# The last output tile of a gated-attention and MLP kernel, split at column 288 instead of column 192

## The chip, the cores and the metric

The kernel runs on one core of one Trainium2 chip. The metric is the device time of one execution in microseconds. A core has five engines that run side by side and wait for each other through semaphores: TensorE (PE in the profile; its weight loads are shown apart as PEld) multiplies matrices into PSUM, VectorE (DVE), ScalarE (ACT) and GpSimd (POOL) work on tiles, and SyncE (SP) here only issues DMA transfers. ACT and POOL can issue transfers too. A transfer is cut into packets that 16 DMA engines move.

## The reference

Two stages follow each other. The first is a linear attention with a decaying state, for 4 batches, 8 heads, 768 steps and a head size of 48; the second is an MLP on the 3,072 rows that come out of it, with 384 model columns, 2,048 hidden columns and a gate h * cos(h):

```
for t in range(S):
    state = alpha[:, :, t, :, None] * state + np.einsum('bhd,bhe->bhde', k[:, :, t], v[:, :, t])
    y[:, :, t] = np.einsum('bhd,bhde->bhe', q[:, :, t], state)
...
x = np.ascontiguousarray(attn_out.transpose(0, 2, 1, 3)).reshape(B * S, H * D)
...
h = x @ w_in
g = h * np.cos(h)
return (g @ w_out).astype(np.float32)
```

The output is 3,072 by 384 in fp32. Matrices are multiplied in bf16 and summed in fp32.

## The kernel before

The 3,072 rows are worked in 12 pairs of 128-row chunks (J = 0 to 11, three pairs a batch). For each pair the attention steps (sums of the logarithms of alpha, scaled q and k, transposes, scores, mask, outer products, the running state, and the output `yT`) make x transposed in bf16, and then the MLP follows in three kinds of steps:

- `mlp1` (the matmuls at L360) makes the hidden layer in four pieces of 512 columns in PSUM. `cosine` (L366, on ACT) and `gate` (L371, on DVE) turn each piece into bf16 tiles `gsb`, with the hidden columns on the partitions.
- `mlp2` (L389) multiplies the 16 blocks of 128 hidden columns with `w2` and sums them into one PSUM tile of 128 rows by 384 columns for each chunk c = 0, 1 of a pair. The step is split into four parts of four blocks each, so that a part can start as soon as its piece of the gate is there. Each matmul has a 128x128 block of `gsb` as its stationary weights, which PEld loads before it, and streams columns of `w2`.
- `evict_o` (L401) copies the tile out of PSUM on ACT or DVE, and `store` (L407) issues its transfer to the output on SP's queue, 1,536 bytes a row.

The very last tile, (J, c) = (11, 1), is made otherwise. It lies in two PSUM tiles of different banks, `o_last`, with half the columns each. Each part of `mlp2` runs its four blocks for the first half and then the same four blocks for the second (L381 to L384), so the block of weights is loaded once for each half. `evict_o` copies the first half on ACT and the second on DVE (L397), and `store` issues the first on ACT's own queue and the second on SP's.

The order of the work is written out by hand. `PLAN` gives each step of each pair a time, the steps are sorted by it, and every engine and every queue carries out its share in that order. Times in `PLAN` only order the steps. For the end of the program they give, on TensorE, for pair 11: `m2 0 1`, `m2 1 1`, `m2 0 2`, `m2 0 3`, `m2 1 2`, `m2 1 3` (chunk, part), so the last 16 matmuls are the parts 2 and 3 of the last tile. Then come `evo 0`, `out 0`, `evo 1` and `out 1`. After the last store SP waits for all outstanding transfers, and a closing exchange of semaphores between the engines ends the program.

Two other places are used below for their durations: `cums` and `cums0` end in matmuls of only two columns (L168), each with a weight block of 128x128, and the inputs are loaded with rows of 384 bytes.

Of the kernel before, what the change touches and what calls it, by code (L numbers as in the profile page):

```python
# [9 lines left out]
FP = mybir.dt.float32  # L10
# [6 lines left out]
def kernel(  # L17
# [10 lines left out]
    nc = tc.nc  # L28
    B, H, S, D = q.shape
    DM, DF = moe_w_in.shape  # L30
    C = 128
# [16 lines left out]
    sb = ctx.enter_context(tc.tile_pool(name="sb", bufs=2))  # L48
# [31 lines left out]
    for lst, nm, n in ((lna_t, "lna", NL), (kh_t, "kh", NQ), (qh_t, "qh", NQ), (vp_t, "vp", NV)):  # L80
        for r in range(n):
            t = consts.tile([C, 2, H, 64], BF, tag=f"{nm}{r}", name=f"{nm}{r}")
            nc.vector.memset(t[:, :, :, D:64], 0.0)
            lst.append(t)
    for r in range(NS):
        t = consts.tile([C, 2, H, 64], BF, tag=f"vs{r}", name=f"vs{r}")
# [8 lines left out]
    w2 = consts.tile([C, NF, DM], BF, tag="w2", name="w2")  # L95

    a_sb, kqv, cp_sb, icp_sb, qkT_sb, A_sb, c2_sb = {}, {}, {}, {}, {}, {}, {}
    xT, gsb = {}, {}
# [73 lines left out]
    def two_banks(name):  # L172
        return ps.tile([C, 2, 512], FP, tag="h", name=name, bufs=3)
# [179 lines left out]
    h_ps, c_sb, o_ps, o_sb = {}, {}, {}, {}  # L353
# [17 lines left out]
        nc.vector.tensor_tensor(out=gsb[J][:, u * FW : (u + 1) * FW], in0=h_ps.pop((J, u)), in1=c_sb.pop((J, u)),  # L371
                                op=ALU.mult)

    HALVES = [slice(0, DM // 2), slice(DM // 2, DM)]

    def mlp2(J, c, part):
        if (J, c) == (NJ - 1, 1):
            if part == 0:

                o_ps[J, c] = [ps.tile([C, 512], FP, tag="x", name="o_last", bufs=1), two_banks("o_last")[:, 0]]  # L380
            for z, cols in enumerate(HALVES):  # L381
                for ft in range(part * NF // MP, (part + 1) * NF // MP):
                    nc.tensor.matmul(o_ps[J, c][z][:, 0 : DM // 2], gsb[J][:, ft, c * C : (c + 1) * C], w2[:, ft, cols],  # L383
                                     start=(ft == 0), stop=(ft == NF - 1))  # L384
            return
        if part == 0:
            o_ps[J, c] = ps.tile([C, 512], FP, tag="o", name="o_ps", bufs=1)
        for ft in range(part * NF // MP, (part + 1) * NF // MP):
            nc.tensor.matmul(o_ps[J, c][:, 0:DM], gsb[J][:, ft, c * C : (c + 1) * C], w2[:, ft],  # L389
                             start=(ft == 0), stop=(ft == NF - 1))  # L390

    def evict_o(J, c, copy):
        if (J, c) == (NJ - 1, 1):
            o_sb[J, c] = []
            for z, cp in enumerate((nc.scalar.copy, nc.vector.tensor_copy)):
                t = sb.tile([C, DM // 2], FP, tag=f"o_half{z}", name="o_half", bufs=1)
                cp(out=t, in_=o_ps[J, c][z][:, 0 : DM // 2])  # L397
                o_sb[J, c].append((t, HALVES[z], (nc.scalar, nc.sync)[z]))
        else:
            t = sb.tile([C, DM], FP, tag="o_sb", name="o_sb", bufs=4)  # L400
            copy(out=t, in_=o_ps.pop((J, c))[:, 0:DM])  # L401
            o_sb[J, c] = [(t, slice(0, DM), nc.sync)]
# [8 lines left out]
    def idle(n):  # L411
# [13 lines left out]
        "evT": lambda J, c, eng="DVE": evict_T(J, c, copies[eng]), "scores": scores, "mask": mask, "outer": outer,  # L425
        "add": add_state, "state": decay_state, "yT": yT, "evy": lambda J, c, eng="ACT": evict_y(J, c, copies[eng]),
        "m1": mlp1, "sin": cosine, "gate": gate, "m2": mlp2, "evo": lambda J, c, eng="ACT": evict_o(J, c, copies[eng]),
        "out": store, "idle": idle,
    }
# [73 lines left out]
    for key, line in PLAN.items():  # L503
        kind, *rest = key.split()
        for J, word in enumerate(line.split()):
            if word != "-":
                t, _, eng = word.partition(":")
# [38 lines left out]
```

## Time and profile before

| | us |
|---|---|
| median of 3 runs | 184.79 |
| lowest and highest | 184.72, 184.88 |
| the profiled execution | 185.2 |
| its span, from the first to the last instruction | 183.4 |
| PE, DVE, ACT, POOL busy | 177.0, 128.4, 129.4, 80.3 |
| mlp1 matmuls L360 (576), mlp2 matmuls L389 (368) | 67.1, 67.4 |
| the last tile's 32 matmuls L383 | 3.1 |
| its copies L397 on ACT and on DVE | 0.32, 0.36 |

The profile is of one execution. A line of a group names the source line, the engine, the operation and the tiles as out<-in, then shapes and count; after the bar stand the busy time in us, the mean duration of one in ns, and the idle time before them with what ended it. Matmuls overlap, so the mean of one (246 ns at L383) is longer than the step from one to the next, which is read from the chain: so many us for so many matmuls. The chain is followed back from the last instruction, at each step to what released it. A view in order of time gives start and duration of each instruction or run of like instructions; SPq and ACTq are the queues' issues of transfers. The granted TensorE clock was 1.000 throughout.

### The profile page before, as it was taken

The numbers are of one execution on the slowest core, as the hardware profiler recorded it, in microseconds if no ns is written. First come the engines' busy times: TensorE is split into PE (matmuls) and PEld (weight loads), VectorE is DVE, ScalarE is ACT, GpSimd is POOL, SyncE is SP. The second block draws the span as 40 slices with busy tenths as digits, with TensorE's granted clock in tenths as the row PEclk, the third lists the DMA queues.
The fourth block names the chain that finished last, engine by engine and source line by source line (L and its number), as shares of the span: only waits on it lengthen the run. The fifth ranks groups of instructions, "written<-read, shape, count | busy, mean of one in ns | idle before, by whom it ended". The sixth has DMA issues, their size and how long they took to land.

```text
span 183.4 us, 5752 instructions
## 1 busy us (share of the span) xinstructions
PE 177.0 (96%) x2473; PEld 132.8 (72%) x2473; DVE 128.4 (70%) x174; ACT 129.4 (71%) x168; POOL 80.3 (44%) x114
## 2 busy tenths in 40 slices
PE   7999999989999999989999999999999999999993
PEld 2444889664797876966789769776786796788772
DVE  7268879179889696689539985988569759074650
ACT  3665769698599989869798999659947173551531
POOL 5357500568687756562991099345075111000000
DMA  6999999999988999989228970571652300020122
GB/s 151 261 261 198 215 211 249 246 267 287 247 197 201 262 242 230 256 189 285 59 46 211 282 212 4 138 176 32 168 162 65 98 5 0 5 86 4 43 86 86
DMA packets 57801, 29.47 MB, mean 161 GB/s; under 512 B 50992, under 2 KB 56496, under 8 KB 57776
## 3 DMA queue, kind: packets, MB, share of 16 engines
q1 hardware_dynamic: 56256, 25.86, 57.7%
q0 software_dynamic: 1376, 3.15, 9.1%
q8 instruction: 19, 0.31, 0.7%
q10 hardware_dynamic: 144, 0.10, 0.2%
q14 instruction: 6, 0.05, 0.1%
HBM read 25.17 MB, written 4.72 MB: 163 GB/s over the span
## 4 chain that ended last, share of the span: by engine, by line
PE 87%; ACT 8%; DMA 2%; DVE 1%; issue 1%
PE h_ps L360 34%; PE o_ps L389 31%; PE y_ps L339 5%; PE A_ps L273 4%; PE idle_ps L415 3%; PE T_ps L259 3%; PE U_ps L290 2%; DMA a<-in_alpha_dram 2%; ACT c_sb L366 2%; ACT lna L142 2%; PE o_last L383 1%; ACT cp L201 1%; PE cums_h L156 1%; PE cums L156 1%; ACT icp L193 1%; ACT L137 1%
## 5 line engine op out<-in xcount | busy, mean ns | idle before, releaser
L371 DVE TENSOR_TENSOR gsb<-h_ps,c_sb 128x1024 bf16<-128x1024 f32 x48 | 58.1, 1222 | 24.1 <-ACT c_sb L366 22.8
L366 ACT ACTIVATE c_sb<-h_ps,halfpi 128x1024 bf16<-128x1024 f32 x48 | 52.8, 1113 | 24.1 <-PE h_ps L360 21.7
L389 PE MATMUL o_ps<-w,gsb 128*128 128x384 bf16 x368 | 67.4, 327 | 1.1 <-DVE gsb L371 0.8
L360 PE MATMUL h_ps<-xT,w 128*128 128x256 bf16 x576 | 67.1, 273 | 0.1
L360 PEld LDWEIGHTS <-w 128*128 128x128 bf16 x576 | 62.4, 114 | 2.7 <-issue 0.4
L389 PEld LDWEIGHTS <-gsb 128*128 128x128 bf16 x368 | 33.8, 98 | 22.1 <-DVE gsb L371 1.4
L312 POOL TENSOR_TENSOR un<-us,c 128x384 bf16<-128x384 f32 x20 | 16.7, 835 | 42.5 <-DVE us L304 27.6
L278 DVE TENSOR_TENSOR A_sb<-A_ps,msk 128x1024 bf16<-128x1024 f32 x24 | 28.8, 1216 | 2.7 <-PE A_ps L273 2.7
L217 POOL TENSOR_TENSOR qh<-q,cp 128x384 bf16<-128x384 f32 x21 | 20.9, 1004 | 12.3 <-PE A_ps L273 8.1
L213 POOL TENSOR_TENSOR kh<-k,icp 128x384 bf16<-128x384 f32 x17 | 17.0, 1006 | 0.7 <-ACT icp L193 0.7
L150 POOL TENSOR_TENSOR a<-a 128x384 f32<-128x384 f32 x9 | 9.0, 1000 | 15.0 <-DMA a<-in_alpha_dram 14.8
L415 PE MATMUL idle_ps<-zeros 128*128 128x512 bf16 x44 | 12.9, 428 | 1.2 <-DVE zeros L52 1.2
L265 DVE COPY qkT<-T_ps 128x1024 bf16<-128x1024 bf16 x14 | 9.3, 682 | 5.0 <-PE T_ps L259 5.0
L137 ACT ACT_TABLE_LOAD x9 | 11.5, 1283 | 0.9 <-PEq L530 0.7
L142 ACT ACTIVATE lna<-a 128x768 bf16<-128x768 f32 x12 | 10.1, 845 | 2.8 <-DMA a<-in_alpha_dram 2.8
L265 ACT COPY qkT<-T_ps 128x1024 bf16<-128x1024 bf16 x10 | 9.8, 1017 | 2.9 <-PE T_ps L259 1.6
L220 POOL CAST vp<-v 128x768 bf16<-128x768 f32 x12 | 9.9, 825 | 4.1 <-DMA v<-in_v_dram 4.1
L366 ACT ACT_TABLE_LOAD x9 | 11.5, 1283 | 0.2
L401 ACT COPY o_sb<-o_ps 128x384 f32<-128x384 f32 x12 | 5.8, 482 | 8.2 <-PE o_ps L389 8.2
L304 DVE TENSOR_TENSOR us<-U_ps,un 128x384 f32<-128x384 f32 x16 | 8.8, 551 | 2.5 <-PE U_ps L290 1.4
L350 ACT CAST xT<-y_ps 128x384 bf16<-128x384 f32 x14 | 7.6, 597 | 4.0 <-PE y_ps L339 3.4
L401 DVE COPY o_sb<-o_ps 128x384 f32<-128x384 f32 x11 | 6.1, 552 | 6.2 <-PE o_ps L389 6.2
(70 smaller groups left out, 153.1 us busy)
## 6 DMA issues: line engine op xcount, KB each, us to landing
a<-in_alpha_dram SPq DMA_DIRECT2D x12, 384.0 KB, 5.9
q<-in_q_dram SPq DMA_DIRECT2D x12, 384.0 KB, 5.4
k<-in_k_dram SPq DMA_DIRECT2D x12, 384.0 KB, 5.9
v<-in_v_dram SPq DMA_DIRECT2D x12, 384.0 KB, 5.9
out_dram<-o_sb SPq DMA_DIRECT2D x23, 192.0 KB, 2.1
vs<-vp SPq DMA_DIRECT2D x36, 64.0 KB, 2.5
w<-in_moe_w_in_dram POOLq DMA_DIRECT2D x2, 768.0 KB, 9.8
w<-in_moe_w_out_dram POOLq DMA_DIRECT2D x4, 384.0 KB, 9.1
```

The source lines that it names most:

```text
L137: nc.scalar.preload_act_table_set("natural_log_exp_and_others")
L142: nc.scalar.activation(out=lna_t[J % NL][:, :, :, 0:D].rearrange("p e h d -> p h e d"), in_=a_sb.pop(J), func=AF.Ln)
L213: eng.tensor_tensor(out=kh_t[J % NQ][:, e, :, 0:D], in0=kqv["k", J][:, :, e], in1=icp_, op=ALU.mult)
L217: eng.tensor_tensor(out=qh_t[J % NQ][:, e, :, 0:D], in0=kqv["q", J][:, :, e], in1=cp, op=ALU.mult)
L265: copy(out=qkT_sb[J][:, c], in_=T_ps[J][:, c].rearrange("r n e s -> r n (e s)"))
L278: nc.vector.tensor_tensor(out=A_sb[J][:, c].rearrange("s a p t -> s (a p) t"), in0=A_ps.pop((J, c)).rearrange("s a p t -> s (a p) t"), in1 ...
L312: nc.gpsimd.tensor_tensor(out=u, in0=U_sum.pop(n), in1=c2_sb[J][:, :, c].unsqueeze(3).to_broadcast([C, NP, 2, D]), op=ALU.mult)
L360: nc.tensor.matmul(h_ps[J, u][:, f, :], cols, xT[J][:, kk, :], start=(kk == 0), stop=(kk == KT - 1))
L366: nc.scalar.activation(out=c_sb[J, u], in_=h_ps[J, u], func=AF.Sin, bias=halfpi, scale=1.0)
L371: nc.vector.tensor_tensor(out=gsb[J][:, u * FW : (u + 1) * FW], in0=h_ps.pop((J, u)), in1=c_sb.pop((J, u)), op=ALU.mult)
L389: nc.tensor.matmul(o_ps[J, c][:, 0:DM], gsb[J][:, ft, c * C : (c + 1) * C], w2[:, ft], start=(ft == 0), stop=(ft == NF - 1))
L415: nc.tensor.matmul(idle_ps[0], zeros[:, 0:C], zeros, start=True, stop=True)
```

## The change

The last output tile is split at column 288 instead of column 192. The first part then has 288 columns and goes by ACT's copy and ACT's queue; the second has 96 columns and goes by DVE's copy and SP's queue. The order of all steps, the two PSUM banks, the number of instructions and the total of columns and bytes stay as they are. Rows of the two stores have 1,152 and 384 bytes instead of 768 and 768. The two tiles in SBUF get new names and sizes, 1,152 and 384 bytes a partition.

```diff
-    HALVES = [slice(0, DM // 2), slice(DM // 2, DM)]
+    PARTS = [slice(0, 288), slice(288, DM)]
...
-            for z, cols in enumerate(HALVES):
+            for z, cols in enumerate(PARTS):
                 for ft in range(part * NF // MP, (part + 1) * NF // MP):
-                    nc.tensor.matmul(o_ps[J, c][z][:, 0 : DM // 2], gsb[J][:, ft, c * C : (c + 1) * C], w2[:, ft, cols],
+                    nc.tensor.matmul(o_ps[J, c][z][:, 0 : cols.stop - cols.start], gsb[J][:, ft, c * C : (c + 1) * C], w2[:, ft, cols],
                                      start=(ft == 0), stop=(ft == NF - 1))
...
             for z, cp in enumerate((nc.scalar.copy, nc.vector.tensor_copy)):
-                t = sb.tile([C, DM // 2], FP, tag=f"o_half{z}", name="o_half", bufs=1)
-                cp(out=t, in_=o_ps[J, c][z][:, 0 : DM // 2])
-                o_sb[J, c].append((t, HALVES[z], (nc.scalar, nc.sync)[z]))
+                n = PARTS[z].stop - PARTS[z].start
+                t = sb.tile([C, n], FP, tag=f"o_part{z}", name="o_part", bufs=1)
+                cp(out=t, in_=o_ps[J, c][z][:, 0:n])
+                o_sb[J, c].append((t, PARTS[z], (nc.scalar, nc.sync)[z]))
```

## The prediction

> **What bounds the kernel now.** I read the busy shares first, then the end of the chain that ended last, the three engines and the queue that close the program, the stores, and at last the rows that price narrow matmuls and narrow transfers. The busy shares:
>
> ```profile
> PE 177.0 (96%) x2473; PEld 132.8 (72%) x2473; DVE 128.4 (70%) x174; ACT 129.4 (71%) x168; POOL 80.3 (44%) x114
> ```
>
> TensorE carries the span (183.4 us at a granted clock of 1.000). The change touches only the last output tile, so the chain's end decides (start, us, what):
>
> ```profile
> 176.30 0.72 PE o_ps L389 x4
> 177.02 0.66 PE o_last L383 x8
> 177.68 1.30 PE o_ps L389 x8
> 178.98 1.33 PE o_last L383 x16
> 180.31 0.02 issue
> 180.34 0.36 DVE o_half L397
> ```
>
> From 176.3 us TensorE runs without a gap; then one copy on VectorE, then the store. The engines' and queues' own order of time around that:
>
> ```profile
> 179.02 0.48 ACT L401 COPY o_sb<-o_ps 128x384 f32<-128x384 f32 x1 [2.88 <-PE o_ps L389]
> 180.01 0.32 ACT L397 COPY o_half<-o_last 128x192 f32<-128x192 f32 x1 [0.51 <-PE o_last L383]
> 180.35 0.37 ACTq L407 DMA_DIRECT2D out_dram<-o_half  x1
> ...
> 179.52 0.33 SPq L407 DMA_DIRECT2D out_dram<-o_sb  x1
> 180.72 0.33 SPq L407 DMA_DIRECT2D out_dram<-o_half  x1
> ```
>
> The first half is copied and issued by ACT 0.37 us before SP issues the second half (180.72 less 180.35). Both copies find their engine idle. The stores of these last microseconds, from issue to landing:
>
> ```profile
> out_dram<-o_sb SPq DMA_DIRECT2D x1, 192.0 KB, 1.9
> out_dram<-o_half ACTq DMA_DIRECT2D x1, 96.0 KB, 1.7
> out_dram<-o_half SPq DMA_DIRECT2D x1, 96.0 KB, 1.6
> ```
>
> Before rounding, ACT's 1.7 is 1.69 and SP's 1.6 is 1.64, so ACT's half lands at 182.04 and SP's at 182.36, and 1.05 us of closing follow to 183.4. The last landing sets the end. How full the 16 DMA engines are then (after the busy times of PE, PEld, DVE, ACT and POOL: clock, DMA share, GB/s; the first line is the last 192 KB store, the second the two halves, the third the 384-byte loads in mid-kernel):
>
> ```profile
> 180.40:180.80 0.40, 0.00 (x0) 0.00 (x0) 0.29 (x1) 0.00 (x0) 0.00 (x0) 1.00 0.97 365
> ...
> 181.60:181.80 0.20, 0.00 (x0) 0.00 (x0) 0.00 (x0) 0.00 (x0) 0.00 (x0) 1.00 0.94 311
> ...
> 66.00:68.00 2.00, 2.00 (x16) 1.36 (x14) 2.00 (x2) 1.71 (x3) 0.52 (x1) 1.00 1.07 278
> ```
>
> One packet's time is its bytes x 16 x share / rate: 1,536 bytes 65 ns, 768 bytes 37 ns, 384 bytes 24 ns. The engines are nearly full while a store moves, so whether two stores follow each other or fall together matters.
>
> **Part 1: the matmuls (L383), 16 of 192+192 columns to 16 of 288+96.** In the chain one of 192 columns steps 1.33/16 = 83 ns, one of 384 columns 1.30/8 = 163 ns. Between them lie 0.417 ns a column and 3 ns each, so 288 columns step 123 ns and 96 columns 43 ns: 166 ns for the pair, as before. The stream costs 0, if the load of each 128x128 weight block stays hidden behind the 43 ns. Two rows bear on that; the chain early in the kernel and the groups:
>
> ```profile
> 6.12 0.19 PE cums_h L168 x8
> ...
> L168 PEld LDWEIGHTS <-lna 128*128 128x128 bf16 x60 | 3.3, 96 | 1.4
> ...
> L383 PEld LDWEIGHTS <-gsb 128*128 128x128 bf16 x32 | 2.7, 98 | 0.4
> ```
>
> At L168 each 2-column matmul has its own full weight block, and eight take 0.19 us: 24 ns each, load included. That is under 43, so the load should stay hidden. The bounds: nothing gained (columns stream at the same rate), and at worst the recorded 98 ns of one load as the step, (98 - 43) x 16 = 0.88 us, of which 0.06 is absorbed: the L389 matmul at 176.19 waits for the last `gate`, some 0.06 us after the stream before it is over. I take 0, since L168 is nearest in its weight load and 98 ns overlaps even there.
>
> The Trainium skill, page "TensorE: Matmul & The Clock Gate", section "Back-to-back issue gap", gives about 81 ns for a pair of weight load and 128-column matmul in a sustained stream, longer than its columns take; by it the 16 narrow ones would cost up to (81 - 43) x 16 = 0.61 us more, an estimate. The 24 ns of L168 speak against it here.
>
> **Part 2: when each part is ready.** The last matmul ends where it did, so the DVE copy still starts at 180.34. The last four matmuls of the first part end one tail of 4 x 43 ns before that, no longer 4 x 83: 0.16 us later. The ACT copy starts at 180.17.
>
> **Part 3: the copies (L397).** ACT takes 0.48 us for 384 columns and 0.32 for 192, so 0.40 for 288: it ends at 180.57. DVE takes 0.55 (the 11 copies at L401 of 552 ns) and 0.36, so 0.26 for 96: it ends at 180.60, 0.10 earlier. No work is queued on either engine behind them. The tiles' bytes per partition sum to the same 1,536, so nothing else moves in memory.
>
> **Part 4: the stores (L407).** Issue follows a copy by 0.03: ACT's (144 KB) at 180.60, 0.24 later; SP's (48 KB) at 180.63, 0.10 earlier. They were staggered by 0.37 and now fall together. Nothing waits behind either on its queue except SP's closing waits, which need both. Two prices for the pair:
> - As one store. The two make up the same 192 KB as the last full tile, whose landing came 1.87 after its issue (the 1.9 of the row, before rounding; from 179.52 to 181.39): 180.61 + 1.87 = 182.48, or 0.12 later than 182.36.
> - With the packets. Each of 16 engines has 8 rows. A row in one packet takes 65 ns; in two, 51 (1,152 bytes, on the line between 37 and 65) plus 24, so 75: 8 x 10 = 0.08 us more. ACT's issue takes 0.04 longer than SP's (0.37 and 0.33). With some of both, 182.48 becomes up to 182.60: 0.24 later.
>
> I take the middle, +0.18. Below: if each store lands as fast as its half did (ACT 180.60 + 1.69 = 182.29), -0.07. Above: if a 384-byte store packet takes as long as a full row (65 ns instead of 24), 8 x 41 = 0.33 us more, so +0.51. No store of 384-byte rows is in this trace; the 384-byte loads are the nearest row by size, which is why 24 is taken.
>
> The same skill, page "DMA: Bandwidth & Descriptors", section "Specifications", puts the least transfer for full rate at 512 bytes and says that below it the DMA engine reads, modifies and writes. The loads at 384 bytes reach 278 GB/s here, but no narrow store tests it.
>
> **The sum.** Matmuls 0, DVE's chain -0.10, the landing turned from SP's lone store to the meeting of both: net +0.18. On the profiled execution, 185.2 us (183.4 span and 1.8 around it), that is 185.4. That execution lies 0.41 above the median of the runs; the step is carried over unscaled: 184.79 + 0.18 = 184.97.
>
> **The rivals.** About 0.2%, 0.37 us, is what a measurement of this kernel can tell from no change.
> - *Narrow matmuls held by their weight loads* (slower). A step over 55 ns adds (55 - 43) x 16 = 0.19 and with the stores' 0.18 passes 0.37. Priced at 70 ns, midway between 43 and 98: 0.43 - 0.06 + 0.18 = +0.55, 185.34; at 98 ns 185.79. For it: 98 ns is what a load is recorded with. Against: the 24 ns steps. Chance 0.17. The skill's 81 ns, named above, lies inside it.
> - *Narrow store rows* (slower). The 384-byte store packets cost a full row's 65 ns: +0.51, 185.30; it passes 0.37 from 24 + 0.19/8 = 48 ns. For it: two stores now compete, and the narrow one issues last. Against: loads of that size at 24 ns. Chance 0.20. The skill's line on 512 bytes would act this way.
> - *The stores don't hinder each other* (a small gain). ACT's lands at 182.29, SP's before it: 184.79 - 0.07 = 184.72, still no measurable change. For it: 37 ns a packet leaves the engines at 0.94, not 1. Against: ACT's is half as large again. Chance 0.10.
> - *A gain over 0.2%.* All that the change can free is DVE's 0.10 and what the narrower SP store saves, 8 x (37 - 24) = 0.10: together 0.20, short of 0.37, and ACT's store would have to vanish. Chance 0.05, for what I have not seen.
>
> **How the numbers follow.** The forecast, both stores meeting at +0.1 to +0.25, has 0.45 and is the predicted time; 0.03 I leave to small losses that add up past 0.37. Faster: 0.05. Within 0.2%: 0.45 + 0.10 = 0.55. Slower: 0.17 + 0.20 + 0.03 = 0.40. The range begins at 184.70, under the third rival, and reaches to 185.40, over the second and the first at 70 ns; it leaves out 0.05 below, and above it half of the first rival and a little of the second, 0.12.
>
> **What would show it.** In the profile of the changed kernel: L383 in two forms whose pair of eights in the chain still takes 0.66 us; L397 at about 0.40 on ACT and 0.26 on DVE, starting near 180.17 and 180.34; both L407 issues within 0.05 us of each other at about 180.6; the last landing near 182.55. Wrong it would be if the chain's L383 pieces grow (first rival), if the SP store lands later than 1.95 after its issue (second), or if the last landing comes before 182.36 (third).

## The result, and the profile after

The changed kernel takes 185.34 us (median of 11 runs) against 184.88 us for the kernel before, run beside it (11 runs): a ratio of 1.0022, with a 95% interval from 1.0012 to 1.0033, or 0.41 us (0.22 to 0.61). It is slower, by about as much as can be told from no change. The median lies inside the range given, 184.70 to 185.40, and 0.37 above the predicted 184.97; against the 184.79 that the prediction started from, the predicted step was +0.18.

The end of the chain in the changed kernel (start, us, what):

```profile
176.08 0.72 PE o_ps L389 x4
176.80 0.66 PE o_last L383 x8
177.46 1.30 PE o_ps L389 x8
178.76 1.33 PE o_last L383 x16
180.10 0.02 issue
180.12 0.26 DVE o_part L398
```

The matmul pieces are as long as before to the last digit, 0.66, 1.30 and 1.33 us. VectorE's copy is 0.10 shorter. This execution happens to reach the last tile 0.22 us sooner than the profiled one of before, through work far ahead of the change: from 21 to 79 us of the span its matmuls run about 0.3 us later than those of before, and from 81 us on they run 0.22 us sooner throughout. So the two are laid over each other at the start of VectorE's last copy (180.34 before, 180.12 after), which follows the last matmul at the same distance in both. I call what lies between it and the end of the span the closing stretch. The groups of the changed lines, mean ns of one after the busy time:

```profile
L383 PE MATMUL o_last<-w,gsb 128*128 128x288 bf16 x16 | 2.6, 286 | 0.0
L383 PEld LDWEIGHTS <-gsb 128*128 128x128 bf16 x32 | 2.6, 98 | 0.8
L383 PE MATMUL o_last<-w,gsb 128*128 128x96 bf16 x16 | 1.3, 206 | 0.0
L398 ACT COPY o_part<-o_last 128x288 f32<-128x288 f32 x1 | 0.4, 400 | 0.7 <-PE o_last L383 0.7
L398 DVE COPY o_part<-o_last 128x96 f32<-128x96 f32 x1 | 0.3, 257 | 2.9 <-PE o_last L383 2.9
```

The copies and issues in order of time, and the last stores from issue to landing:

```profile
179.95 0.40 ACT L398 COPY o_part<-o_last 128x288 f32<-128x288 f32 x1 [0.67 <-PE o_last L383]
180.12 0.26 DVE L398 COPY o_part<-o_last 128x96 f32<-128x96 f32 x1 [2.94 <-PE o_last L383]
180.38 0.39 ACTq L408 DMA_DIRECT2D out_dram<-o_part  x1
180.41 0.33 SPq L408 DMA_DIRECT2D out_dram<-o_part  x1
```

```profile
out_dram<-o_sb SPq DMA_DIRECT2D x1, 192.0 KB, 1.9
out_dram<-o_part ACTq DMA_DIRECT2D x1, 144.0 KB, 2.0
out_dram<-o_part SPq DMA_DIRECT2D x1, 48.0 KB, 1.7
```

The stores are issued 0.03 us apart and ACT's lands last, 2.0 us after its issue. SP's own waits show the same. First the kernel before, then the changed one (waiter, what for, total us, times, longest):

```profile
SPq L541 <- DMA out_dram<-o_half: 0.9, 2, 0.6
```

```profile
SPq L542 <- DMA out_dram<-o_part: 1.1, 1, 1.1
```

Before, SP waits twice, first for ACT's half and then 0.3 us more for its own. Now it waits once, for ACT's store, and its own is there already when it comes to it.

How full the 16 DMA engines are in the changed kernel while both stores move:

```profile
181.40:181.60 0.20, 0.00 (x0) 0.00 (x0) 0.00 (x0) 0.00 (x0) 0.00 (x0) 1.00 0.98 305
181.60:181.80 0.20, 0.00 (x0) 0.00 (x0) 0.00 (x0) 0.00 (x0) 0.00 (x0) 1.00 1.06 377
```

They are full (0.98 and 1.06, where the halves had 0.94). By the packet times of the trace a row of 1,152 bytes takes 51 ns and one of 384 bytes 24 ns.

In unrounded times, from the start of VectorE's copy, the last landing moved from 2.03 us (SP's half) to 2.25 (ACT's 288 columns), and the closing stretch from 3.09 to 3.38 us: 0.29 in all, of which 0.06 lies behind the last landing (1.06 before, 1.13 after; the difference is 0.063).

### The profile page after: what moved, and what is told of

The parts are those of the page before. It is cut to its first block, busy times and chain, and to the rows that moved or that the text cites. A ratio compares the mean times of both kernels' runs of the same rounds, so it can differ in the third digit from the quotient of the medians.

```text
span 183.5 us, 5752 instructions
## 1 busy us (share of the span) xinstructions
PE 177.4 (97%) x2473; PEld 132.7 (72%) x2473; DVE 128.3 (70%) x174; ACT 129.5 (71%) x168; POOL 80.5 (44%) x114
## 3 DMA queue, kind: packets, MB, share of 16 engines
q0 software_dynamic: 1376, 3.15, 9.2%
## 4 chain that ended last, share of the span: by engine, by line
PE 88%; ACT 7%; DMA 2%; issue 1%; DVE 0%
PE h_ps L360 34%; PE o_ps L389 31%; PE y_ps L339 5%; PE A_ps L273 4%; PE idle_ps L416 3%; PE T_ps L259 3%; PE U_ps L290 2%; DMA a<-in_alpha_dram 2%; ACT lna L142 2%; PE o_last L383 1%; PE cums_h L156 1%; ACT cp L201 1%; ACT c_sb L366 1%; PE cums L156 1%; ACT icp L193 1%; ACT L137 1%
```

## The experiments

The theory after this reading: the loss is 0.29 us and lies in the two stores, which meet on full DMA engines, plus one closing wait. The rivals: rows of 384 bytes or narrow matmuls are costly in themselves; or something ahead of the closing stretch costs as well. Every number named "after the copy" counts from the start of VectorE's last copy.

**The changed kernel again, twice.** No edit; each time beside the kernel before.

> The changed kernel once more, beside the kernel before. In the two profiles the stretch from the start of VectorE's last copy to the end of the span (called the closing stretch here) took 3.09 us before and 3.38 us after, all else in the program being the same work. Theory (the loss is in the stores alone): the closing stretch is 3.36 to 3.40 us again and the time is 0.16% above the kernel before. Rival (something ahead of the closing stretch costs too, so that the measured 0.22% is more than the stores): the closing stretch is 3.38 again but the time is 0.22% or more above.

> The changed kernel a third time, on the chip of the two late versions. Theory (0.29 us in the stores, nothing elsewhere): closing stretch 3.36 to 3.40 us, ratio to the kernel before 1.0016. Rival (a loss ahead of the closing stretch as well): the same closing stretch, ratio 1.0022 or more.

Measured: closing stretch 3.40 and 3.39 us, so the profiles of the changed kernel agree to 0.02 (the kernel before left one profile, of 3.09). The ratios were 0.9998 (0.9977 to 1.0019) and 1.0023 (1.0005 to 1.0041). The first interval holds 1, that is no change, and the theory's 1.0016, but not the rival's 1.0022; the second repeats the loss and holds both figures. Weighted by their intervals, the three ratios make about 1.0018, or 0.34 us, between the two figures.

The profiles say more. From the start of the last tile's first matmul, where the change begins, to the start of VectorE's last copy, 4.86 us pass in the kernel before and in all three profiles of the changed one, so nothing between them costs. The profile's 0.29 is enough for the measured loss; a further 0.1 us in the work ahead of the last tile, whose code is the same in both kernels, is neither shown nor excluded.

**One store left out, then the other.**

```diff
-        for t, cols, eng in o_sb.pop((J, c)):
+        for t, cols, eng in o_sb.pop((J, c))[:1]:
```

```diff
-        for t, cols, eng in o_sb.pop((J, c)):
+        for t, cols, eng in o_sb.pop((J, c))[-1:]:
```

> The changed kernel without the store of its 96-column part, so columns 288 to 383 of the last 128 output rows are left out; all matmuls and copies stay. Theory (ACT's store lands late because it shares the DMA engines with SP's): ACT's 144 KB lands 1.75 to 1.80 us after its issue, in place of 1.99, and the closing stretch is 3.05 to 3.15 us in place of 3.38. Rival (144 KB at 1,152 bytes a row is that slow by itself): 1.95 us or more, closing stretch above 3.28.

> The changed kernel without the store of its 288-column part, so columns 0 to 287 of the last 128 output rows are left out; all matmuls and copies stay. Theory (a 384-byte row in a store is no dearer than one in a load, 24 ns a packet, and alone the narrow store is the quickest): it lands 1.48 to 1.56 us after its issue, and the closing stretch is 2.84 to 2.96 us. Rival (a store of rows under 512 bytes takes the time of a full row): 1.64 us or more, closing stretch 2.98 us or more.

The two profiles' last stores, the wide one alone and the narrow one alone:

```profile
out_dram<-o_part ACTq DMA_DIRECT2D x1, 144.0 KB, 1.8
```

```profile
out_dram<-o_part SPq DMA_DIRECT2D x1, 48.0 KB, 1.5
```

Alone, the wide store lands 1.79 us after its issue, against 1.99 beside the narrow one: the meeting costs it 0.20 us. The narrow one lands 1.52 after its issue alone, sooner than the half of 768-byte rows (1.64), and its packets take 22 ns. Both are where the theory put them, and the rivals on size and on short rows fall. The first closing stretch, 3.19 us, missed its 3.05 to 3.15: 1.14 us lie behind the landing and not 1.06, because one more of SP's waits still follows. The second was 2.94, as expected.

**The stores named in the other order.**

```diff
-        for t, cols, eng in o_sb.pop((J, c)):
+        for t, cols, eng in o_sb.pop((J, c))[::-1]:
```

> The changed kernel with its last two stores named in the other order in the program, SP's 96 columns first; they are on different queues, so their issue times should stay. At the end SP waits for each store in that order. Theory (with ACT's store last to land, one more of SP's waits lies behind it, 0.06 us): the closing stretch is 3.32 us in place of 3.38. Rival (the order of the waits costs nothing): 3.36 to 3.40 us.

The closing stretch stayed at 3.38, where the theory had 3.32. But the edit did not do what it was for: in the trace SP still waits for ACT's store first and for its own after it. So this run says nothing about the cost of the order.

**The queues exchanged.**

```diff
-                o_sb[J, c].append((t, PARTS[z], (nc.scalar, nc.sync)[z]))
+                o_sb[J, c].append((t, PARTS[z], (nc.sync, nc.scalar)[z]))
```

> The changed kernel with the queues of its last two stores exchanged: SP issues the 288 columns that ACT copied, ACT's queue the 96 columns that VectorE copied. The stores still meet. Theory (SP's last waits come in a fixed order, ACT's store ahead of its own, so a last landing on ACT's queue leaves one more wait of 0.06 us behind it): the wide store lands as late as before, within 0.03 us, and the closing stretch is 3.28 to 3.34 us in place of 3.38. Rival (the order of the waits costs nothing): 3.36 to 3.40 us.

```profile
180.91 0.33 SPq L408 DMA_DIRECT2D out_dram<-o_part  x1
180.94 0.37 ACTq L408 DMA_DIRECT2D out_dram<-o_part  x1
```

```profile
out_dram<-o_part SPq DMA_DIRECT2D x1, 144.0 KB, 1.7
out_dram<-o_part ACTq DMA_DIRECT2D x1, 48.0 KB, 1.9
```

The closing stretch was 3.25 us, under the range expected, because the wide store did not land as late as before: it came at 2.01 after the copy and the narrow one last, at 2.18. SP's store went first in both kernels. In the changed one both stores paid: the narrow one took 1.7 us where alone it took 1.5, and the wide one 2.0 for 1.8. Here only ACT's narrow one did, with 1.9 for the 1.5 that it took alone on SP's queue. The theory's fixed order did not hold either: SP waited for its own wide store first and for ACT's narrow one after it, so the order did not go with the queue. The narrow store lands last here and is waited for last, and 1.08 us lie behind it.

**One store in place of two.**

```diff
-                t = sb.tile([C, n], FP, tag=f"o_part{z}", name="o_part", bufs=1)
-                cp(out=t, in_=o_ps[J, c][z][:, 0:n])
-                o_sb[J, c].append((t, PARTS[z], (nc.scalar, nc.sync)[z]))
+                if z == 0:
+                    t = sb.tile([C, DM], FP, tag="o_part", name="o_part", bufs=1)
+                cp(out=t[:, PARTS[z]], in_=o_ps[J, c][z][:, 0:n])
+            o_sb[J, c] = [(t, slice(0, DM), nc.sync)]
```

> The changed kernel's matmuls and copies, but both copies write one tile of 384 columns that SP stores at once, 1,536 bytes a row in one packet. The closing stretch took 3.09 us in the kernel before and 3.38 in the changed one. Theory (of the 0.29 us, 0.20 is two stores meeting, of which the doubled number of packets is a part, and 0.06 the extra wait behind ACT's store): issue at 0.28 after the start of VectorE's copy, landing 1.85 to 1.90 after that, closing stretch 3.18 to 3.24 us. Rival (any way of moving 192 KB this late costs the same): 3.34 us or more.

The store was issued at 0.32 and landed 1.87 us later, as expected of it, at 2.19. The closing stretch was 3.33, a miss by 0.09: the issue came 0.04 later, as it now waits for both copies, and 1.14 us lie behind the landing, since one more wait follows here too. That is 0.01 short of the rival's 3.34, and the rival is nearly what was seen: one store of full rows lands only 0.06 sooner than two that meet. Most of the loss is that all 192 KB start this late, whatever they are cut into.

**A smaller shift, 240 and 144 columns.**

```diff
-    PARTS = [slice(0, 288), slice(288, DM)]
+    PARTS = [slice(0, 240), slice(240, DM)]
```

> The change at a smaller size: 240 and 144 columns, order and queues as in the changed kernel. Issues should come at 0.14 (ACT) and 0.34 us (SP) after the start of VectorE's copy, 0.20 apart, where the kernel before has 0.37 and the changed one 0.03. Theory (the 16 engines have 584 ns of packets from the first store's start on, so the last landing is late by how little the stores are staggered): last landing 2.06 to 2.12 us after the start of the copy and closing stretch 3.12 to 3.20 us. Rival (the cost is in rows under 512 bytes, which 144 columns, 576 bytes, do not have): 3.04 us or less, since VectorE's copy is 0.05 shorter than before.

The issues came at 0.14 and 0.33, the last landing at 2.11, the closing stretch took 3.19 us: within the theory's range at its upper end. Rows of 576 bytes lose too, so the loss isn't bound to 512 bytes. SP's narrow copy and narrow store should have gained 0.05 and more; its packets, though, began 1.01 us after its issue, where SP's half of the kernel before took 0.84; ACT's packets had begun 0.32 us ahead of them.

**The split of the change, with the stores moved apart.** Part 0 of the last tile stays; parts 1 to 3 of the narrow piece run behind the wide piece's last. The sum of TensorE's work is the same.

```diff
-                for ft in range(part * NF // MP, (part + 1) * NF // MP):
+                first, parts = (part, 1) if z == 0 or part == 0 else (1, MP - 1 if part == MP - 1 else 0)
+                for ft in range(first * NF // MP, (first + parts) * NF // MP):
```

> The changed kernel's own split, 288 and 96 columns, with the narrow part's matmuls of parts 1, 2 and 3 all at the very end: only the moment at which the wide part is ready moves, to 12 steps of 43 ns = 0.52 us before the last matmul, so ACT's store is issued some 0.09 us before VectorE's copy starts and SP's 0.29 after. Theory (the loss is that the stores meet, not their shapes): SP's store is the last to land, 1.85 to 1.95 us after the start of VectorE's copy, and the closing stretch is 2.92 to 3.02 us, in place of 3.38 in the changed kernel and 3.09 before; the time is 0.04 to 0.1% under the kernel before. Rival (rows of 384 bytes, or 16 narrow matmuls in a row, cost by themselves): 3.15 us or more.

```profile
178.93 1.50 PE o_last L384 x20
180.43 0.02 issue
180.46 0.26 DVE o_part L399
```

```profile
180.38 0.37 ACTq L409 DMA_DIRECT2D out_dram<-o_part  x1
180.46 0.26 DVE L399 COPY o_part<-o_last 128x96 f32<-128x96 f32 x1 [2.94 <-PE o_last L384]
180.74 0.33 SPq L409 DMA_DIRECT2D out_dram<-o_part  x1
```

```profile
out_dram<-o_part ACTq DMA_DIRECT2D x1, 144.0 KB, 1.8
out_dram<-o_part SPq DMA_DIRECT2D x1, 48.0 KB, 1.6
```

With the issues 0.37 us apart, as in the kernel before, the last landing is SP's at 1.90 and the closing stretch 2.96 us: 0.42 less than in the changed kernel, with the same 288 and 96 columns, the same rows and the same queues. So the loss is a matter of the time at which the stores start, and not of narrow rows or narrow matmuls in themselves. This run moves the start of the wide store and the meeting at once; the run with the wide store alone parts them (alone it lands at 2.05, 0.03 later than SP's half did in the kernel before; the meeting adds 0.20).

The ratio to the kernel before is 1.0001 (0.9986 to 1.0016), where 0.9990 to 0.9996 was expected; the interval holds the gain and no gain. Against the changed kernel, which ran on the same chip, the time does tell: medians of 185.03 and 185.61 us, 12 runs each, 0.3% less (0.1 to 0.4% when the runs of both are resampled).

**The same order with 256 and 128 columns, and with halves.** The edit is the one above, with `PARTS` cut at 256 for the first (run twice), and in the kernel before for the second.

> A split at 256 and 128 columns, and the narrow part's matmuls of parts 1, 2 and 3 all run at the very end, behind the wide part's last: the wide part is then ready 12 steps of 56 ns = 0.67 us before the last matmul, ACT's store is under way before SP's starts, and VectorE's copy and SP's store are narrow. Theory (the meeting of the stores is what costs; the narrow copy and narrow store are gains that the meeting ate): the closing stretch is 2.93 to 3.00 us, 0.09 to 0.16 under the kernel before, SP's store lands 1.55 to 1.60 after its issue, and the time is 0.05 to 0.09% below the kernel before. Rival (rows under 768 bytes are costly in SP's store, or the narrow matmuls are): 3.09 us or more, the time at or above the kernel before.

> The late version with 256 and 128 columns again, beside the changed kernel on one chip. Theory: closing stretch 2.92 to 2.96 us; the ratio to the kernel before is 0.9992 (0.15 us), and the time lies 0.24% under the changed kernel's. Rival (other work, such as the part of the last tile that no longer fills TensorE early, eats the gain): the closing stretch is 2.94 us, but the ratio to the kernel before is 1.000 or above.

> The kernel before, halves of 192 columns, with the second half's matmuls of parts 1, 2 and 3 all at the very end, as in the 256 and 128 version, whose closing stretch was 2.94 us. ACT's store is then issued about 1 us before SP's. Theory (halves were staggered enough before, so moving the first one further away frees little, and the gain of the 256 and 128 version needs the narrower second part): the closing stretch is 3.05 to 3.09 us. Rival (the later order alone makes the gain): 2.98 us or less.

With 256 and 128 columns the closing stretch was 2.94 us and then 2.97 (0.01 over its range; so two profiles of one kernel can differ by 0.03), SP's store landing 1.56 and 1.58 after its issue; the ratios were 0.9981 (0.9960 to 1.0001) and 0.9993 (0.9978 to 1.0009). In the profile it is 0.12 to 0.15 us better than the kernel before; in the time that is too little to tell. Against the changed kernel on the same chip the first set is 0.15% faster (185.43 and 185.72 us), and the second 0.20% (185.24 and 185.61), where 0.24% was expected. With halves the closing stretch stayed at 3.09, so the later order alone gains nothing: halves were far enough apart, and the gain comes from the narrower last copy and store, once these have the DMA engines to themselves.

The closing stretches side by side. Landing is the moment at which SP's wait for the store that lands last is over; times in us from the start of VectorE's last copy, the first column how much later SP's queue is given its store than ACT's:

| kernel | SP's issue less ACT's | last landing | behind it | closing stretch |
|---|---|---|---|---|
| before | 0.37 | 2.03 (SP) | 1.06 | 3.09 |
| changed | 0.03 | 2.25 (ACT) | 1.13 | 3.38 |
| 240 and 144 | 0.20 | 2.11 (SP) | 1.08 | 3.19 |
| queues exchanged | -0.04 | 2.18 (ACT) | 1.08 | 3.25 |
| 288 alone | - | 2.05 | 1.14 | 3.19 |
| 96 alone | - | 1.81 | 1.14 | 2.94 |
| one store | - | 2.19 | 1.14 | 3.33 |
| 288 and 96, late | 0.37 | 1.90 (SP) | 1.07 | 2.96 |
| 256 and 128, late | 0.59 | 1.87 (SP) | 1.06 | 2.94 |
| halves, late | 1.03 | 2.02 (SP) | 1.08 | 3.09 |

The stretch behind the last landing has two lengths: 1.06 to 1.08 us where the store that lands last is also the last of the two that SP waits for, 1.13 to 1.14 where one more wait follows it. That is the 0.06 that the reordering run failed to test; it is read across these kernels and not from one that changes this alone. The trace of the changed kernel agrees: SP's wait for ACT's store is over at 2.252 us and its next wait, for its own store, which had landed at 2.00, at 2.314.

## Why the prediction was right, and where it was short

*Part 1, the matmuls at no cost.* Right. A matmul of 96 columns steps 42 to 43 ns by the starts in the trace, and the chain's pieces did not grow. The first rival, weight loads that show, falls. The 81 ns of the Trainium skill's page "TensorE: Matmul & The Clock Gate", section "Back-to-back issue gap", does not hold for this stream either: load and matmul take half of that here, as the 24 ns of L168 had said, and with 128 columns, the width for which the page gives it, the run with 256 and 128 columns steps 55 to 56 ns.

*Part 2 and part 3, readiness and copies.* Right to 0.01 us. ACT's copy began 0.17 ahead of VectorE's, as 180.17 and 180.34 had it, and the copies took 400 and 257 ns for the 0.40 and 0.26 worked out.

*Part 4, the stores.* The mechanism was right: the issues fell together (0.03 apart, as predicted), the pair then landed late, and neither short rows nor absent contention explains the time. Which store lands last the prediction had not said; it was ACT's. The size was short in two terms. I had put the landing at 0.12 later by the one price and up to 0.24 by the other and took 0.18; it was 0.23, near the price that counts the packets. And a term was missing: I named SP's closing waits but let the 1.05 us of closing stand as it was, though ACT's store is waited for ahead of SP's and its landing last leaves one more wait behind it, 0.06 us. 0.23 + 0.06 = 0.29, where 0.18 was predicted. Split by the runs in another way: the wide store alone lands 0.03 later than SP's half did, the meeting adds 0.20, the wait 0.06.

*The rivals.* The narrow store rows fall on the 1.5 us of the narrow store alone and on its packets of 22 to 24 ns; beside the wide one it took 1.7, under the 1.95 named as the sign. The line on 512 bytes in the Trainium skill's page "DMA: Bandwidth & Descriptors", section "Specifications", names a read and a write back below that size; no such cost is seen here, 24 ns for 384 bytes being less than the 36 for 768, though more per byte. The rival without hindrance falls on 2.0 us against 1.8 alone.

*The chances.* I gave 0.55 to a change within 0.2% and 0.40 to a loss beyond it. The ratio, 1.0022, lies just beyond that border and its interval holds both sides. That the range held the median was in part luck: it was drawn up to 185.40 for two rivals, priced at 185.34 and 185.30, that the profile then rejected, and the forecast itself, +0.1 to +0.25, was passed by the profile's 0.29 and by the 0.41 of the ratio. The time alone, 185.34, would have fitted the first rival exactly; only the profile tells them apart. What is left open is the 0.1 us between the 0.29 and the 0.41: the interval of the ratio, 0.22 to 0.61 us, holds both.

## What to carry to other kernels

When two transfers close a program, shortening the last one is worth nothing if that moves the other into it: price the pair as one transfer from the moment at which both are issued (which fell 0.1 us short here), and make the larger one ready well ahead. Here the same split lost 0.29 us or gained 0.13 in the closing stretch, by nothing but the time at which the wide part was ready. And check in which order the end of the program waits, as well as what it waits for.

## What the runs showed of the hardware that was not expected

Of two stores issued within 0.04 us of each other, SP's moved first in all five runs, though ACT's issue had begun first in four of them. SP's issue was also the first to end in all five (in the changed kernel 0.62 us after the start of the copy, ACT's 0.65), and in every run with two stores the one whose issue ended first moved first; so a preference for SP's queue is not shown. In the changed kernel SP's packets began 0.83 us after its issue and ACT's 0.97, although SP's issue came 0.03 later; ACT's issue itself took 391 to 396 ns there in four profiles, and 369 to 372 in all the others.

How the two then shared the engines differed. In the changed kernel they moved side by side: SP's 48 KB moved for 0.47 us, against 0.31 alone, while ACT's packets had begun 0.12 us behind them. With the queues exchanged, ACT's 48 KB began only 1.18 us after their issue, 0.38 us into the 0.54 us that SP's 144 KB moved, so there the second store largely waited its turn. And with 240 and 144 columns, where ACT's was first by 0.20 us, it was SP's that began late (1.01 us). No run shows the rule behind these three cases.
